# Four late MoE blocks: 32x32 turns on DVE and sixteen small array tiles instead of TensorE transposes

## The chip, the cores and the metric

The kernel runs on one core of a Trainium2 chip. The metric is the device time of one execution in microseconds (us). The engines are PE (TensorE: matmuls and weight loads), DVE (VectorE), ACT (ScalarE), POOL (GpSimd) and SP (SyncE, which here issues all DMAs from one in-order queue). Matmul results land in PSUM, which has 8 banks; everything else lives in SBUF.

## The reference

Three layers run one after another, all in float32.

```
attn = softmax(rope(q) rope(k)^T / 8) v        # 4 batches, 8 heads, 576 positions, 64 per head
x    = attn as [2304 tokens, 512]
h    = x @ w_in;  g = max(h,0) + alpha*min(h,0)     # [2304, 2048]
y    = g @ w_out                                    # [2304, 512]
logits = y @ phi                                    # [2304, 32 slots]
d = softmax of logits over the tokens;  slot_in = d^T @ y      # 32 slots: 8 experts x 4
slot_out[e] = relu(slot_in[e] @ w1[e]) @ w2[e]
out = softmax of logits over the slots @ slot_out
```

The kernel never forms y for all tokens. Since y = g @ w_out, the logits are g @ (w_out phi), and slot_in is (d^T g) @ w_out. So for each block of tokens it needs the sums over tokens of d (32 slots) times g (2048 features): the slots' sums. They are added up over the blocks with a running maximum, as in a streaming softmax.

## The kernel before

**Blocks.** The 2304 tokens are nine blocks of 256: two per batch (0 to 7) and one made of the four batches' last 64 tokens (8). A block's MoE work is 16 chunks of 128 features. A chunk is `mm1` (12 fp16 matmuls of 128x256 into the tile `ph`, line 734), then ACT `rl` (line 742) and DVE `g` (line 747), which read `ph` and free its PSUM bank. g then lies with features on the partitions and tokens along the free side. Three PSUM banks ("pm") serve `ph`, all transposes and most other results.

**Turning g.** The slots' sums contract over tokens, so tokens must lie on the partitions. After every second chunk PE makes four 128x128 transposes (`pt`, line 753) into a "pm" bank and ACT copies them to SBUF (`gt`, line 758): 8 such groups per block. After every fourth chunk come the logits (`lg`, line 764).

**Dispatch of a block** (`dispatch_events`): DVE scales the logits (`lp`, line 802), PE spreads them to 128 partitions (`lgt`, line 806), DVE takes the maximum (`sts`, line 827) and a copy (`lt`, line 816), ACT makes the fading factor (line 836) and the exponentials (`edt`, line 840), PE turns these (`pd`, line 845), DVE scales them (`dn`, line 850 or 852), PE makes the slots' sums (`pu`, line 858: 8 matmuls of 512 columns in four column tiles of the array, 32 slots by 512 features each), and DVE adds them to the running sum (`sacc`, line 867).

**After the last block**: `pa` turns the sum (line 1078), `at` scales it, `px` multiplies by w_out (line 1090), `pst` turns that (line 1100), and the experts follow: `ph` of line 1126 with w1, `po` of line 1180 with w2, and the output. The expert weights (33.5 MB) and w_out (8 MB) are fetched once attention has ended, into whatever SBUF tiles have come free: the pools "x" (26 tiles), "xt" (4), "w" (4) and "raw" (3 tiles, which also hold `gt`). w_out arrives as float64 and DVE converts it to fp32 in three operations for each of 16 pieces (`wo`, lines 986, 988 and 990).

**Order.** Every operation is given an engine, a cost, a due time, the operations it depends on and the buffers it takes. `Plan.order` plays this through with those costs and due times; the order in which operations start there becomes the program's order on each engine. On the chip each engine works through its list in order and waits on semaphores. MoE blocks run beside the attention of the next batch; when attention ends, part of block 5 and blocks 6 to 8 remain.

Of the kernel before, what the change touches and what calls it, by code (L numbers as in the profile page):

```python
# [11 lines left out]
F32 = mybir.dt.float32  # L12
# [3 lines left out]
ALU = mybir.AluOpType  # L16
AX = mybir.AxisListType
# [8 lines left out]
NS = E * SL  # L26
NT = B * S
BLK = 256
HALF = D // 2
NB, NW, WO_AT, MOVED = 13, 7, 12, 1  # L30

# [131 lines left out]
def attn_moe_softmoe(ctx, tc, qx, kx, vx, w_in, w_out, alpha, phi, w1, w2, tab, msks, w_out_t, out):  # L163
    nc = tc.nc
# [556 lines left out]
    def chunk_events(f, blk, due):  # L721
# [67 lines left out]
    def dispatch_events(ib, blk, due):  # L789
# [79 lines left out]
        def gather_s():  # L869
            if first:  # L870
                nc.vector.tensor_copy(ssum, st[:, 2:3])
            else:
                nc.vector.scalar_tensor_tensor(ssum, ssum, st[:, 1:2], st[:, 2:3], ALU.mult, ALU.add)

        s_e, s_pd, s_dn, s_pu = Slot("edt"), Slot("pm"), Slot("dn"), Slot("pm")
        s_lt, s_ln = Slot("lt"), Slot("pm")
# [7 lines left out]
        done.append(op(DVE, 131, d + 1, kept_l, [x], uses=[s_ln]))  # L884
        o = op(PE, 160, dp, turn_d, [o], takes=[s_pd], uses=[s_e, s_pd])
        o = op(DVE, 131, d, turned_d, [o], takes=[s_dn], uses=[s_pd, s_dn])
        o = op(PE, 1720, dp, slots, [o] + blk["gt_op"], takes=[s_pu], uses=[s_dn, s_pu] + list(blk["s_gt"].values()))
        a = op(DVE, 750, d, gather, [o, fd, run["sum"]], uses=[s_pu])
        run["gathered"] = a
        run["sum"] = op(DVE, 130, d, gather_s, [ex, fd, a])  # L890
        done.extend([a, run["sum"]])


    done = []
# [42 lines left out]
    for ib in range(9):  # L937
        if ib < 8:
            b, u = divmod(ib, 2)
            blk = {"x": xts[b, u], "inv": [(0, BLK, viv[b][:, 0:1])], "inv_op": [viv_op[b]]}  # L940
        else:
            blk = {"x": xts["tail"], "inv": [(64 * b, 64 * b + 64, viv[b][:, 0:1]) for b in range(B)], "inv_op": [tk_op]}
        blks.append(blk)
    for ib, blk in enumerate(blks):
# [24 lines left out]
    def late_w(f):  # L969
# [22 lines left out]
        d = 990 + 0.1 * f  # L992
        o = order_ops["wo"] = op(DMA, 1456, d, load, [att_done, order_ops.get("wo")], takes=[s_raw], uses=[s_raw])
        o = op(DVE, 450, d, lambda: conv(0), [o, wo_op.get(j)], takes=[] if z else [s_wo[j]], uses=u)
        o = op(DVE, 750, d, lambda: conv(1), [o], uses=u)
# [11 lines left out]
    for base in range(0, len(order), 4):  # L1007
        for half in range(2):
            for i in range(base, base + 4):
# [26 lines left out]
                for cut in range(n):  # L1036
                    due = 1000 + base + 2 * half + 0.2 * (i - base) + (2 * cut if n > 1 else 0)
                    ops.append(op(DMA, 1456 * len(parts) / n, due, lambda cut=cut, load=load: load(cut),
                                  [att_done, blks[8]["turn"] if slot.cls == "raw" else None] + ops[-1:],
                                  takes=[] if cut else [slot], uses=[slot]))  # L1040
# [27 lines left out]
    for j in range(2):  # L1068
        hz_zero.append(op(POOL, 900, 1000, lambda j=j: zero(j), [att_done], takes=[s_hz[j]], uses=[s_hz[j]]))
    sr = cst.tile([128, 2], F32, name="sr")  # L1070
# [4 lines left out]
    def turn_a():  # L1075
        fin["pa"] = ps_m.tile([128, 4, 4, NS], F32, tag="pm", name="pa")
        for c in range(4):
            nc.tensor.transpose(fin["pa"][:, c].rearrange("p g s -> p (g s)"), run["acc"][:, 128 * c:128 * c + 128], idf)

    def turned_a():  # L1080
        fin["at"] = fin["p"].tile([128, 4, 4, NS], F32, name="at")
        for c in range(4):
            iv = inv_w[:].rearrange("p (g h) -> p h g", h=2)[:, c // 2]
            nc.vector.tensor_tensor(fin["at"][:, c], fin["pa"][:, c], iv.unsqueeze(2).to_broadcast([128, 4, NS]), ALU.mult)

# [15 lines left out]

    o = op(PE, 430, D2 - 200, turn_a, [run["gathered"]], takes=[s_pa], uses=[s_pa])
    o = op(DVE, 600, FIRST, turned_a, [o, fin_open], uses=[s_pa])
# [303 lines left out]
```

## Time and profile before

| what | value |
|---|---|
| runs | 670.12, 674.26, 674.0 us; median 674.0 us |
| the profiled execution's own time | 673.49 us |
| its span, first to last instruction | 671.6 us |
| mean granted TensorE clock | 0.963 of full |
| PE busy | 611.0 us, 91% of the span |
| DVE busy | 456.0 us, 68% |
| ACT busy | 360.5 us, 54% |

The profile is one execution. Busy shares are means over stages: attention with MoE blocks beside it until about 508 us, then MoE blocks alone until about 600 us, then the dispatch of the last block, the experts and the output. What a change in one stage is worth has to be read from that stage: from the chain of waits (the work that ended last, followed back) and from the busy time of each engine in stretches of time. PEclk is the granted clock as a share of 2.4 GHz. The mean of a matmul's duration contains its way through the array, so matmuls that follow each other closely take less time than the sum of their durations. An fp32 matmul shows as two records in the trace.

### The profile page before, as it was taken

Reading aid. Unit: us, or ns where it says so; the run is one execution under the profiler, and the core shown is the slowest. Engines: PE = TensorE matmul, PEld = TensorE weight load, DVE = VectorE, ACT = ScalarE, POOL = GpSimd, SP = SyncE. Lnnn points to the kernel's source line nnn. Section 1 sums busy time; section 2 is a strip of 40 time slices with the busy share of each in tenths; the row PEclk is TensorE's granted clock in tenths of the full one; section 3 lists DMA queues with packets and bytes.
Section 4 is the critical chain, followed back from the end, with each engine's and each line's share of the span. In section 5 each row is a group of like instructions: output and inputs, shape, how many; then the busy total and the mean of one; then the engine's idle time right before and its main releaser. Section 6 shows DMA issues by size and latency. Waiting matters only on the chain.

```text
span 671.6 us, 13543 instructions
## 1 busy us (share of the span) xinstructions
PE 611.0 (91%) x5072; PEld 433.9 (65%) x5072; DVE 456.0 (68%) x989; ACT 360.5 (54%) x868; POOL 287.8 (43%) x283
## 2 busy tenths in 40 slices
PE   2879968979999999999999999999999999988984
PEld 1545444545888678686767868777776868753452
DVE  4776798787878777877576787677736884334332
ACT  2536545645687686775757676684643434330211
POOL 0698999374647656466353655522320000000000
PEclk9898988978999999999999999999999999999997
DMA  8954274530489796877867784777576984447998
GB/s 294 372 182 136 78 238 135 167 112 15 148 253 271 252 242 191 241 196 214 245 182 216 211 250 134 220 193 205 158 189 252 410 333 150 149 149 301 356 395 295
DMA packets 72672, 146.57 MB, mean 218 GB/s; under 512 B 8352, under 2 KB 37536, under 8 KB 72608
## 3 DMA queue, kind: packets, MB, share of 16 engines
q1 hardware_dynamic: 72608, 145.72, 68.3%
q8 instruction: 40, 0.66, 0.4%
q14 instruction: 24, 0.20, 0.1%
HBM read 108.73 MB, written 29.88 MB: 206 GB/s over the span
## 4 chain that ended last, share of the span: by engine, by line
PE 71%; DVE 9%; DMA 7%; POOL 6%; ACT 4%; SPq 2%; issue 2%; DVEq 0%; ACTq 0%; POOLq 0%
PE ph L734 26%; PE pv L573 13%; PE st L431 7%; PE pt L753 4%; DMA xw<-in_moe_w_dram 4%; PE lg L764 3%; PE pu L858 3%; POOL e L473 3%; PE st L418 3%; PE pt L494 2%; PE pc L537 1%; PE ph L1126 1%; PE rest L267 1%; DMA vt<-in_v_dram 1%; PE st L427 1%
## 5 line engine op out<-in xcount | busy, mean ns | idle before, releaser
L473 POOL TENSOR_SCALAR e<-e,mm 128x576 f32<-128x576 f32 x144 | 122.8, 865 | 152.7 <-DVE mm L449 112.1
L734 PE MATMUL ph<-xt,w 128*128 128x256 f16 x1536 | 184.5, 273 | 1.1 <-DVE g L747 0.4
L734 PEld LDWEIGHTS <-w 128*128 128x128 f16 x1728 | 163.9, 98 | 33.4 <-issue 11.8
L436 DVE TENSOR_REDUCE mm<-st 128x1 f32<-128x576 f32 x144 | 106.2, 742 | 27.6 <-PE st L431 21.4
L441 ACT ACTIVATE e<-st,mm 128x576 f32<-128x576 f32 x144 | 106.3, 739 | 29.4 <-DVE mm L436 26.5
L747 DVE SCALAR_TENSOR_TENSOR g<-rl,oma,ph 128x256 f32<-128x256 f32 x144 | 68.2, 474 | 59.6 <-ACT rl L742 59.0
L321 POOL TENSOR_TENSOR xn<-xn,tabs 128x576 f32<-128x576 f32 x60 | 90.3, 1519 | 30.6 <-DMA xn<-in_q_dram 14.9
L742 ACT ACTIVATE rl<-ph 128x256 f32<-128x256 f32 x144 | 55.0, 382 | 88.0 <-PE ph L734 87.6
L431 PE MATMUL st<-ks,qs 128*128 128x288 f32 x384 | 71.7, 314 | 0.3 <-ACT e L441 0.3
L481 DVE STREAM_TRANSPOSE tb<-e 128x512 f32<-128x512 f32 x96 | 66.6, 700 | 3.7 <-POOL e L473 3.0
L573 PE MATMUL pv<-ET,vt 128*64 128x256 f32 x512 | 63.9, 393 | 2.6 <-DVE qs L346 1.2
L418 PE MATMUL st<-ks 64*128 64x288 f32 (+1 forms) x168 | 46.9, 504 | 16.3 <-DVE ks L329 11.5
L431 PEld LDWEIGHTS st<-ks,qs 128*128 128x128 f32 x384 | 54.7, 191 | 4.7 <-issue 2.4
L758 ACT ACTIVATE gt<-pt 128x512 f32<-128x512 f32 x72 | 43.0, 597 | 15.7 <-PE pt L753 14.2
L573 PEld LDWEIGHTS pv<-ET,vt 128*64 128x64 f32 x512 | 35.6, 139 | 24.3 <-issue 6.1
L418 PEld LDWEIGHTS st<-ks 64*128 64x128 f32 (+1 forms) x168 | 26.7, 216 | 30.2 <-DVE ks L329 11.5
L753 PE MATMUL pt<-idf,g 128*128 128x128 f32 x288 | 43.8, 275 | 0.6 <-DVE g L747 0.4
L753 PEld LDWEIGHTS pt<-idf,g 128*128 128x128 f32 x288 | 33.3, 141 | 4.2 <-issue 1.2
L324 POOL TENSOR_TENSOR xn<-xn 128x576 f32<-128x576 f32 x24 | 35.6, 1482 | 0.9
L494 PE MATMUL pt<-idf,e 128*128 128x128 f32 x192 | 33.0, 306 | 3.3 <-POOL e L473 3.1
L494 PEld LDWEIGHTS pt<-idf,e 128*128 128x128 f32 x192 | 25.1, 159 | 15.1 <-POOL e L473 8.1
L349 ACT ACTIVATE ks<-xn 64x576 fp32r<-64x576 f32 x48 | 32.6, 680 | 0.7
(161 smaller groups left out, 840.2 us busy)
## 6 DMA issues: line engine op xcount, KB each, us to landing
sc<-tb SPq DMA_DIRECT2D x48, 512.0 KB, 4.3
ET<-sc SPq DMA_DIRECT2D x96, 256.0 KB, 5.4
xw<-in_moe_w_dram SPq DMA_DIRECT2D x42, 512.0 KB, 10.1
xn<-in_k_dram SPq DMA_DIRECT2D x16, 576.0 KB, 5.0
xn<-in_q_dram SPq DMA_DIRECT2D x16, 576.0 KB, 4.4
wraw<-in_moe_w_in_dram SPq DMA_DIRECT2D x8, 1024.0 KB, 7.1
wraw<-in_w_out_t_dram SPq DMA_DIRECT2D x8, 1024.0 KB, 5.4
wor<-in_moe_w_out_dram SPq DMA_DIRECT2D x16, 512.0 KB, 10.2
```

Of the source, the lines that this page charges most:

```text
L321: eng.tensor_tensor(e["x"][:, w], e["x"][:, w], tabs[:, (0 if z == "q" else 2) + w], ALU.mult)
L418: nc.tensor.matmul(st[to, j, at:at + w], x, k[rows, z:z + w], start=True, stop=True)
L431: nc.tensor.matmul(st[:, j, 0:288], r["q"][:, 768 * h + 128 * s:768 * h + 128 * s + 128].bitcast(F32R), r["k"][:, a, h, ks].bitcast(F32R), ...
L436: nc.vector.tensor_reduce(c["mm"][:, h:h + 1], c["st", h][:, :, 0:288], axis=AX.XY, op=ALU.max, negate=True)
L441: nc.scalar.activation(c["e"][:, h].rearrange("p (a n) -> p a n", a=2), c["st", h][:, :, 0:288], AF.Exp, bias=c["mm"][:, h:h + 1], accum_o ...
L473: nc.gpsimd.tensor_scalar(c["e"][:, h], c["e"][:, h], c["mm"][:, 6 + h:7 + h], 1.0, ALU.mult, ALU.mult)
L481: nc.vector.transpose(out=c["tb"][:, :, h].rearrange("p (q m) j -> p q m j", q=4), in_=c["e"][:, h, 64 * h:64 * h + 512].rearrange("p (m q ...
L494: nc.tensor.transpose(c["pt", h][:, i], c["e"][:, h, 64 * h + 128 * i:64 * h + 128 * i + 128], idf)
L573: nc.tensor.matmul(pv[r], v[k, 4 * h + i if i < 4 else 8], x, start=(i == 0), stop=(i == 4))
L734: nc.tensor.matmul(ph, wi[j][:, wp, kc, 128 * fo:128 * fo + 128], xt[:, xp, kc, :], start=(n == 0), stop=(n == 3 * KC - 1),)
L747: nc.vector.scalar_tensor_tensor(blk["g", j][:, fo, :], c["r"], oma[:, f:f + 1], c["ph"], ALU.mult, ALU.add)
L753: nc.tensor.transpose(c["pt"][:, t, i, :], blk["g", j][:, fo - 1 + i, 128 * t:128 * t + 128], idf)
```

## The change

In blocks 5 to 8 (`LATE = 5`) the transposes on PE and their copies on ACT go. DVE turns two chunks of g at a time with one 128x512 transpose that turns each 32x32 block by itself (`turn_g`, tile `gb`). Tokens then lie on the partitions only inside each strip of 32 partitions: strip a holds the features 32a to 32a+31 of each chunk of 128. So the slots' sums are made strip by strip: `slots_late` has 64 matmuls, each contracting over 32 tokens, on a 32x32 tile of the array. The tile's row strip a is the feature strip, its column strip the output's 32 partitions; the four row strips write into the four banks of the two score tiles ("st"), which attention no longer needs then. The eight groups of 32 tokens are split in pairs over two column strips, so each sum comes as two halves. The exponentials are scaled by DVE while still in rows (`scaled_d`) and turned by DVE too (`blocks_d`), in place of `pd` and `dn`. The running sum gets a new layout, `acc2` (in one of the four "xt" tiles, from the end of attention until `pa`), added to by four DVE operations per block; the first of the four blocks takes the old sum over. `pa` becomes eight matmuls that turn the sum and add the two halves, with a 0/1 matrix `selh`. Around this: the slots' sums of block 5 wait until attention is done (as `acc2` is opened then), one of the two zeroed tiles `hz` is made after `pa`, a w_out piece takes its "x" tile for the result when it is loaded, and expert weights in "raw" tiles may load once block 8 has taken its second `gb` tile.

```
-NB, NW, WO_AT, MOVED = 13, 7, 12, 1
+NB, NW, WO_AT, MOVED, LATE = 13, 7, 12, 1, 5
...
+        def turn_g():
+            if f == 1 or f == 9:
+                blk["gt", j // 2] = wgt.tile([128, 8, BLK], F32, tag="w", name="gb")
+            nc.vector.transpose(
+                out=blk["gt", j // 2][:, f % 8 - 1:f % 8 + 1, :].rearrange("p c n -> p (c n)"),
+                in_=blk["g", j][:, fo - 1:fo + 1, :].rearrange("p c n -> p (c n)"))
...
-        if fo % 2:
+        if fo % 2 and blk["late"]:
+            o = op(DVE, 760, due + 2.5, turn_g, blk["g_op"][-2:] + [raw_done, blk.get("turn")], takes=[s_gt] if f % 8 == 1 else [], uses=[s_g, s_gt])
...
+        def scaled_d():
+            for lo, hi, s in blk["inv"]:
+                nc.vector.tensor_scalar(c["et"][:, lo:hi], c["et"][:, lo:hi], s, None, ALU.mult)
+
+        def blocks_d():
+            nc.vector.transpose(out=c["lp"][:], in_=c["et"][:])
+
+        def slots_late():
+            pu = c["pu"] = [ps_s.tile([128, 2, 512], F32, tag="st", name="pu") for _ in range(2)]
+            for k in range(0, 8, 2):
+                for h in range(2):
+                    for r in range(2):
+                        to = slice(64 * h + 32 * r, 64 * h + 32 * r + 32)
+                        at = slice(32 * (k + r), 32 * (k + r) + 32)
+                        for a in range(4):
+                            rows = slice(32 * a, 32 * a + 32)
+                            nc.tensor.matmul(
+                                pu[a // 2][to, a % 2, 0:256], c["lp"][rows, at], blk["gt", h][rows, :, at],
+                                start=(k == 0), stop=(k == 6), tile_position=(32 * a, to.start))
+
+        def gather_late():
+            if ib == LATE:
+                run["acc2"] = xtp.tile([128, 8, 4, 32], F32, tag="xt", name="acc2")
+            for a in range(4):
+                src = c["pu"][a // 2][:, a % 2, 0:256].rearrange("p (c j) -> p c j", j=32)
+                dst = run["acc2"][:, :, a]
+                if ib > LATE:
+                    nc.vector.scalar_tensor_tensor(dst, dst, st[:, 1:2], src, ALU.mult, ALU.add)
+                    continue
...
+        if ib >= LATE:
+            o = op(DVE, 250 if ib < 8 else 400, d, scaled_d, [o], uses=[s_e])
+            o = op(DVE, 400, d, blocks_d, [o, lg], uses=[s_e, s_lp])
+            s_pu = [Slot("st"), Slot("st")]
+            o = op(PE, 1800, dp, slots_late, [o] + blk["gt_op"], takes=s_pu, uses=[s_lp] + s_pu + list(blk["s_gt"].values()))
...
+            a = op(DVE, 1700, d, gather_late, [o, a, run["sum"]], uses=s_pu + [s_acc2])
...
+    acc2_open = op(None, 0, 0, lambda: None, [att_done], takes=[s_acc2], uses=[s_acc2])
+    for blk in blks[LATE:]:
+        plan.also(blk["slots"], [acc2_open])
...
-        fin["pa"] = ps_m.tile([128, 4, 4, NS], F32, tag="pm", name="pa")
-        for c in range(4):
-            nc.tensor.transpose(fin["pa"][:, c].rearrange("p g s -> p (g s)"), run["acc"][:, 128 * c:128 * c + 128], idf)
+        fin["pa"] = ps_m.tile([128, 8, 2, NS], F32, tag="pm", name="pa")
+        for c in range(8):
+            nc.tensor.matmul(fin["pa"][:, c].rearrange("p h s -> p (h s)"), run["acc2"][:, c].rearrange("p a j -> p (a j)"),
+                             selh[:].rearrange("p h s -> p (h s)"), start=True, stop=True)
...
```

What this does to the order, at three places. **DVE while only MoE blocks run**, in block 8 (`g` is the chunk's second step, `gb` the new turn, `wo` the conversion of w_out; `dn`, `sacc` and `ssum` belong to the dispatch of block 7). Before:

```order
L747 SCALAR_TENSOR_TENSOR g<-rl,oma,ph 128x256
L850 TENSOR_SCALAR dn<-pd,vb 128x64
L747 SCALAR_TENSOR_TENSOR g<-rl,oma,ph 128x256
L867 SCALAR_TENSOR_TENSOR sacc<-sacc,sts,pu 128x512
L873 SCALAR_TENSOR_TENSOR ssum<-ssum,sts 128x1
L747 SCALAR_TENSOR_TENSOR g<-rl,oma,ph 128x256 x11
```

and now, in the last chunks of block 8:

```order
L747 SCALAR_TENSOR_TENSOR g<-rl,oma,ph 128x256
L763 STREAM_TRANSPOSE gb<-g 128x512
L1067 SCALAR_TENSOR_TENSOR wo<-wor,wo 128x512
L747 SCALAR_TENSOR_TENSOR g<-rl,oma,ph 128x256
L1063 TENSOR_SCALAR wo<-wor 128x512
L763 STREAM_TRANSPOSE gb<-g 128x512
L747 SCALAR_TENSOR_TENSOR g<-rl,oma,ph 128x256
L1065 SCALAR_TENSOR_TENSOR wo<-wor,wo 128x512
L747 SCALAR_TENSOR_TENSOR g<-rl,oma,ph 128x256
```

Before, the sixteen conversions were over well ahead of block 8, and `g` stood alone in DVE's list; now turns and conversions stand between the `g` up to the last chunk.

**DVE in the dispatch of block 8**, from the scaled logits to the running sum. Before:

```order
L802 TENSOR_SCALAR lp<-lg,vb 128x64 x4
L827 TENSOR_REDUCE sts<-lgt 128x1
L816 COPY lt<-lgt 32x256
L833 TENSOR_TENSOR sts<-sts 128x1
L824 COPY lall<-ln 128x64
L852 TENSOR_TENSOR dn<-pd,tailk 128x64
L1222 CAST idr<-idf 128x128
L867 SCALAR_TENSOR_TENSOR sacc<-sacc,sts,pu 128x512
```

and now, from the small `sts` on:

```order
L846 TENSOR_TENSOR sts<-sts 128x1
L1065 SCALAR_TENSOR_TENSOR wo<-wor,wo 128x512
L837 COPY lall<-ln 128x64
L1067 SCALAR_TENSOR_TENSOR wo<-wor,wo 128x512
L890 TENSOR_SCALAR edt<-edt,vb 128x64 x4
L1065 SCALAR_TENSOR_TENSOR wo<-wor,wo 128x512
L893 STREAM_TRANSPOSE lp<-edt 128x256
L1067 SCALAR_TENSOR_TENSOR wo<-wor,wo 128x512
L1063 TENSOR_SCALAR wo<-wor 128x512
L1065 SCALAR_TENSOR_TENSOR wo<-wor,wo 128x512
L1067 SCALAR_TENSOR_TENSOR wo<-wor,wo 128x512
L915 SCALAR_TENSOR_TENSOR acc_6270<-acc_6270,sts,pu 128x8x32 x4
```

The last three conversions now lie in this dispatch: two operations ahead of the scaling of the exponentials and one between the scaling and the turn.

**PE at the same place.** Before:

```order
L753 MATMUL pt<-idf,g 128x128 x8
L764 MATMUL lg<-g,wph 32x256 x4
L806 MATMUL lgt<-lp,sel_106 128x256
L821 MATMUL ln<-idf,lt 128x32 x2
L845 MATMUL pd<-idf,edt 128x32 x2
L858 MATMUL pu<-gt,dn 32x512 x8
L1078 MATMUL pa<-idf,sacc 128x128 x4
```

and now:

```order
L771 MATMUL lg<-g,wph 32x256 x4
L819 MATMUL lgt<-lp,sel_106 128x256
L834 MATMUL ln<-idf,lt 128x32 x2
L904 MATMUL pu<-gb,lp 32x256 x64
L1154 MATMUL pa<-selh,acc_6270 128x64 x8
L1169 MATMUL px<-wo,at 32x512 x16
```

The transposes `pt` and `pd` are gone from PE's list in blocks 5 to 8, `pu` has eight times as many matmuls of half the width, and `pa` twice as many.

## Rows read from the trace of the kernel before

**Rows 1.** The page: busy us, share of the span, instructions of PE.
```profile
PE 611.0 (91%) x5072; PEld 433.9 (65%) x5072; DVE 456.0 (68%) x989; ACT 360.5 (54%) x868; POOL 287.8 (43%) x283
```

**Rows 2.** The page: the chain that ended last, share of the span by engine.
```profile
PE 71%; DVE 9%; DMA 7%; POOL 6%; ACT 4%; SPq 2%; issue 2%; DVEq 0%; ACTq 0%; POOLq 0%
```

**Rows 3.** Busy time of each engine in stretches; columns as the first line says.
```profile
core 0: us, PE busy (x) PEld busy (x) DVE busy (x) ACT busy (x) POOL busy (x), PEclk, DMA share, GB/s
475.00:508.00 33.00, 32.85 (x310) 25.22 (x312) 16.33 (x37) 16.01 (x42) 8.40 (x12) 1.00 0.60 157
...
508.00:600.00 92.00, 90.36 (x830) 69.91 (x822) 54.62 (x120) 34.72 (x81) 0.00 (x0) 1.00 0.68 254
515.00:546.00 31.00, 30.18 (x281) 24.41 (x274) 25.73 (x57) 12.03 (x28) 0.00 (x0) 1.00 1.03 410
...
600.00:608.00 8.00, 4.59 (x22) 1.27 (x22) 2.76 (x11) 0.75 (x3) 0.00 (x0) 0.79 0.27 112
```

**Rows 4.** Chain of waits, 575 to 585 us: start us, us, what.
```profile
574.99 0.31 PE pd L845 x2
...
577.25 1.85 PE pu L858 x16
...
580.52 0.44 PE pt L753 x4
```

**Rows 5.** Groups of instructions: count, busy us, mean ns of one, idle before.
```profile
L753 PE MATMUL pt<-idf,g 128*128 128x128 f32 x288 | 43.8, 275 | 0.6 <-DVE g L747 0.4
...
L481 DVE STREAM_TRANSPOSE tb<-e 128x512 f32<-128x512 f32 x96 | 66.6, 700 | 3.7 <-POOL e L473 3.0 <-DMA sc<-tb 0.5
...
L747 DVE SCALAR_TENSOR_TENSOR g<-rl,oma,ph 128x256 f32<-128x256 f32 x144 | 68.2, 474 | 59.6 <-ACT rl L742 59.0
...
L867 DVE SCALAR_TENSOR_TENSOR sacc<-sacc,sts,pu 128x512 f32<-128x512 f32 x8 | 5.9, 741 | 2.0 <-PE pu L858 2.0
...
L986 DVE TENSOR_SCALAR wo<-wor 128x512 int32<-128x512 int32 x16 | 6.3, 420 | 1.2 <-DMA wor<-in_moe_w_out_dram 1.2
...
L988 DVE SCALAR_TENSOR_TENSOR wo<-wor,wo 128x512 int32<-128x512 int32 x16 | 10.8, 683 | 0.0
```

**Rows 6.** Timeline of PE at 59 and at 65 us: start us, us, what, count.
```profile
59.24 1.23 PE L418 MATMUL st<-ks 64*128 64x288 f32 x4
...
65.25 1.25 PE L418 MATMUL st<-ks 64*128 64x288 f32 x8
```

**Rows 7.** Chain of waits, 600 to 616 us: dispatch of block 8 and after.
```profile
600.00 0.87 DVE lp L802 x4
...
600.92 0.71 PE lgt L806 x2
...
601.65 0.42 DVE sts L827
602.08 0.32 DVE lt L816
...
603.92 3.36 PE pu L858 x16
...
608.30 0.67 PE pa L1078 x4
...
608.99 0.30 DVE at L1084
...
609.34 4.23 PE px L1090 x32
...
614.33 1.09 PE pst L1100 x8
```

**Rows 8.** Waits of SP's queue, 595 to 672 us: us in total, times, longest.
```profile
SPq L1033 <- PE pu L858: 9.0, 1, 9.0
SPq L1033 <- PE ph L1126: 7.3, 1, 7.3
```

More of the change, by code (lines that the diff above doesn't have):

```diff
@@ L779, in chunk_events @@
         blk["g_op"].append(o)
-        if fo % 2:
+        if fo % 2 and blk["late"]:
+            o = op(DVE, 760, due + 2.5, turn_g, blk["g_op"][-2:] + [raw_done, blk.get("turn")], takes=[s_gt] if f % 8 == 1 else [], uses=[s_g, s_gt])
+            blk["turn"] = o
+            blk["gt_op"].append(o)
+            if f == 9:
+                blk["turn9"] = o
+        elif fo % 2:
             s_pt = Slot("pm")
@@ L873, in gather_s @@
                 nc.vector.scalar_tensor_tensor(ssum, ssum, st[:, 1:2], st[:, 2:3], ALU.mult, ALU.add)
+        def scaled_d():
[24 more added lines that the diff above has]
+                    continue
+                for z in range(2):
+                    nc.vector.scalar_tensor_tensor(
+                        dst[:, 4 * z:4 * z + 4], run["acc"][:].rearrange("p (c a j) -> p c a j", a=4, j=32)[:, :, a], fz[:, z:z + 1],
+                        src[:, 4 * z:4 * z + 4], ALU.mult, ALU.add)
         s_e, s_pd, s_dn, s_pu = Slot("edt"), Slot("pm"), Slot("dn"), Slot("pm")
@@ L884, in dispatch_events @@
         done.append(op(DVE, 131, d + 1, kept_l, [x], uses=[s_ln]))
[L885 to L888, printed above, removed]
+        if ib >= LATE:
[3 more added lines that the diff above has]
+            o = op(PE, 1800, dp, slots_late, [o] + blk["gt_op"], takes=s_pu, uses=[s_lp] + s_pu + list(blk["s_gt"].values()))
+            blk["slots"] = o
+            a = fd
+            if ib == LATE:
+                a = op(DVE, 75, d, lambda: nc.vector.tensor_tensor(fz, parm, st[:, 1:2].to_broadcast([128, 2]), ALU.mult), [fd, parm_op])
+            a = op(DVE, 1700, d, gather_late, [o, a, run["sum"]], uses=s_pu + [s_acc2])
+        else:
+            o = op(PE, 160, dp, turn_d, [o], takes=[s_pd], uses=[s_e, s_pd])
+            o = op(DVE, 131, d, turned_d, [o], takes=[s_dn], uses=[s_pd, s_dn])
+            o = op(PE, 1720, dp, slots, [o] + blk["gt_op"], takes=[s_pu], uses=[s_dn, s_pu] + list(blk["s_gt"].values()))
+            a = op(DVE, 750, d, gather, [o, fd, run["sum"]], uses=[s_pu])
         run["gathered"] = a
@@ L891, in dispatch_events, with make_par @@
         done.extend([a, run["sum"]])
+    parm = cst.tile([128, 2], F32, name="parm")
+    fz = cst.tile([128, 2], F32, name="fz")
+    selh = cst.tile([128, 2, NS], F32, name="selh")
+    s_acc2 = Slot("xt")
+    def make_par():
+        nc.vector.memset(parm, 0.0)
+        for g in range(4):
+            nc.vector.memset(parm[32 * g:32 * g + 32, g % 2:g % 2 + 1], 1.0)
+    parm_op = op(DVE, 300, 60, make_par)
+    selh_op = op(DVE, 200, 60, lambda: nc.vector.tensor_reduce(
+        selh, idf[:].rearrange("p (h r s) -> p h s r", h=2, s=NS), axis=AX.X, op=ALU.add))
     done = []
@@ L942, in attn_moe_softmoe @@
             blk = {"x": xts["tail"], "inv": [(64 * b, 64 * b + 64, viv[b][:, 0:1]) for b in range(B)], "inv_op": [tk_op]}
+        blk["late"] = ib >= LATE
         blks.append(blk)
@@ L992, in late_w @@
         d = 990 + 0.1 * f
-        o = order_ops["wo"] = op(DMA, 1456, d, load, [att_done, order_ops.get("wo")], takes=[s_raw], uses=[s_raw])
-        o = op(DVE, 450, d, lambda: conv(0), [o, wo_op.get(j)], takes=[] if z else [s_wo[j]], uses=u)
+        o = order_ops["wo"] = op(DMA, 1456, d, load, [att_done, order_ops.get("wo")], takes=[s_raw] if z else [s_raw, s_wo[j]], uses=u)
+        o = op(DVE, 450, d, lambda: conv(0), [o, wo_op.get(j)], uses=u)
         o = op(DVE, 750, d, lambda: conv(1), [o], uses=u)
@@ L1038, in attn_moe_softmoe @@
                     ops.append(op(DMA, 1456 * len(parts) / n, due, lambda cut=cut, load=load: load(cut),
-                                  [att_done, blks[8]["turn"] if slot.cls == "raw" else None] + ops[-1:],
+                                  [att_done, blks[8]["turn9"] if slot.cls == "raw" else acc2_open if slot.cls == "xt" else None] + ops[-1:],
                                   takes=[] if cut else [slot], uses=[slot]))
@@ L1066, in zero @@
         nc.gpsimd.memset(fin["hz", j], 0.0)
-    for j in range(2):
-        hz_zero.append(op(POOL, 900, 1000, lambda j=j: zero(j), [att_done], takes=[s_hz[j]], uses=[s_hz[j]]))
+    hz_zero.append(op(POOL, 900, 1000, lambda: zero(0), [acc2_open], takes=[s_hz[0]], uses=[s_hz[0]]))
     sr = cst.tile([128, 2], F32, name="sr")
@@ L1100, in turn_s @@
             nc.tensor.matmul(fin["pst"][:, c], fin["xs"][:, 128 * c:128 * c + 128], sel4[:, 0], start=True, stop=True)
-    o = op(PE, 430, D2 - 200, turn_a, [run["gathered"]], takes=[s_pa], uses=[s_pa])
+    o = op(PE, 900, D2 - 200, turn_a, [run["gathered"], selh_op], takes=[s_pa], uses=[s_pa, s_acc2])
+    hz_zero.append(op(POOL, 900, 1000, lambda: zero(1), [o], takes=[s_hz[1]], uses=[s_hz[1]]))
     o = op(DVE, 600, FIRST, turned_a, [o, fin_open], uses=[s_pa])
```

4 lines of the change are left out of this document (3 added, 1 removed).

## The prediction

> **What bounds the kernel now.** I read the page first: PE is busy for 91% of the span [rows 1], and 71% of the chain that ended last is PE's [rows 2]. Both are means, so the stages come next. Between 475 and 508 us, where block 5 runs beside the last attention, PE is busy for 32.85 of 33.0 us. Between 508 and 600 us, MoE blocks alone, for 90.36 of 92.0 us, at full granted clock [rows 3]. In both stretches work that leaves PE's list should shorten the time, unless it uncovers another wait. From 600 us on it is different: PE works 4.59 of 8.0 us, and the chain there [rows 7] is a ladder of single operations that hand over between DVE, PE and ACT. What follows hangs on that ladder: SP's queue waits 9.0 us for block 8's `pu`, and later 7.3 us for the experts' first `ph`, before it can fetch more weights [rows 8]. So the end of the kernel moves with the ladder's end, us for us.
>
> **The change, part by part.** All sums are made against the profiled execution's own 673.49 us; the median of the runs shown is 0.5 us higher.
>
> *Transposes.* The 288 records of `pt` [rows 5] are 72 groups of four, 8 per block; four blocks lose 32 groups. One takes 0.44 us of the chain [rows 4]: 14.1 us. Of these, 24 groups (blocks 6 to 8) lie after attention and count fully: 10.6 us. The 8 of block 5 (3.5 us) lie beside attention, whose chain of maximum, exponential and transfers may wait where PE is lighter; I count 2.5. ACT's copies vanish too, worth nothing, as ACT is busy for 34.72 of 92 us [rows 3]. Blocks 5 to 7 also lose `pd`, 0.31 us each on the chain [rows 4]: 0.9.
>
> *The slots' sums.* Now 1.85 us per block [rows 4] for 16 records of 512 columns in four column tiles, four deep: 0.46 us each. The change has 64 matmuls, so 128 records of 256 columns, in sixteen tiles, eight deep. If all sixteen run at once this is 8 x 0.23 = 1.85 us again, and costs nothing. No row shows sixteen. Rows do show two row strips that write the same PSUM partitions in different banks: 4 records of the plain scores take 1.23 us, and 8 records, 4 in each row strip, take 1.25 us [rows 6]. A second strip cost nothing, and column tiles overlap already, so I take 1.85. The other ends: two strips at once 3.7 us, one strip at a time 7.4 us.
>
> The Trainium skill, TensorE: Matmul & The Clock Gate, section Measured speedup vs the span model, gives 10.6 times for sixteen tiles, not 16. By it the slots would take an estimated 64 x 0.46 / 10.6 = 2.8 us, and the sum below would be 4 us worse. The rows on two strips show no such loss.
>
> *DVE.* It gains, for 24 groups after attention, a 128x512 turn each, 0.70 us by the same operation on the exponentials [rows 5]: 16.8 us. The running sum becomes four operations of 256 columns, each like `g` (0.474 us), instead of 0.741 us: 1.2 us more per block, and 3.1 more in block 5, where eight operations take the old sum over. Three conversions (0.42 + 2 x 0.68 each [rows 5], 5.3 us in all) move on into the dispatch of block 8. Busy there was 54.6 us of 92 [rows 3]; now 54.6 + 16.8 + 3.1 + 2.4 - 5.3 = 71.6 in about 81. Who waits: the `g` that frees a `ph` bank now stands behind turns and conversions in DVE's list, and PE's next chunk needs that bank. There are three banks, so a `g` may be late by about a chunk before PE stops. I charge 1.0 us, with 0 and 5.8 as ends; the upper end is worked out as a rival below.
>
> *The ladder at the end.* Before, from `lp` to the start of `at`: 8.99 us [rows 7]. Now: `lp` 0.87, `lgt` 0.71, `sts` 0.42 and `lt` 0.32, as before: 2.3. Then DVE's list holds two conversion steps (2 x 0.68) ahead of the exponentials' scaling, beside ACT's work on the exponentials, which ends sooner: 1.4. The scaling in four pieces as for `lp`: 0.87. Another conversion step ahead of the turn: 0.68. The turn of 256 columns, half of 0.70: 0.35. The slots' sums at the rate that `pu` had here: 3.36, where the granted clock over the stretch was 0.79 [rows 3]. Four additions: 1.9. `pa` is 16 records with 128 columns of weights each, by `pst` (8 in 1.09 us): 2.2. Sum 13.1 us, so 4.1 more than before. If `pu` runs there as it does in warm stretches it is 2.6 more. If PE, with more waiting around it, is still at the lower clock in `pa` and `px` (4.23 us), these double and it is about 10 more; I take 4.1, since the same place before shows only `pu` slowed.
>
> *The rest.* Making `selh` and its like is some microseconds of DVE early on, where PE's chain leads; nothing. The DMA queue has the same bytes after attention; between 508 and 600 us it was busy for 0.68 of the time [rows 3], so fetches that now wait for later conversions have room, at the price of up to one fetch at the end, inside the ladder's bounds.
>
> *Sum.* 10.6 + 2.5 + 0.9 - 4.1 - 1.0 = 8.9 us less: 664.6 against 673.49, and 665 against the median of 674.0. The ends of this case: 661 (all of block 5's groups count, ladder 2.6, no bank waits) and 669 (half of them, ladder 6, bank waits 2).
>
> **The rivals.**
>
> *DVE sets the pace after attention.* For it: its list would be the fullest of all engines. Its densest stretch before held 25.73 us in 31 (0.83), with PE at 30.18 [rows 3]. Its 71.6 us after attention would take 86.3 at that share. PE's way is 92.0 - 10.6 - 0.9 = 80.5, so 5.8 us come back, of which the forecast holds 1.0: 670. Against it: durations of consecutive operations overlap a little, so 0.83 need not be the ceiling.
>
> *The ladder is dearer.* The lower clock holds through `pa` and part of `px`: 5 us more, 670. For it: PE has longer to wait between `lgt` and `pu` than before. Against it: `px` ran warm right after a slowed `pu` before.
>
> *The strips do not run at once.* This is the one that ends on the other side. If row strips shared something (a path into PSUM, the supply of columns), one strip at a time would make `pu` 7.4 us: 4 x 5.55 = 22 more than forecast, 687, slower than now. It decides from 4.1 us per `pu` on, where the four blocks have eaten the 8.9. If only two strips run at once, it is 7.4 us, 672. Against both stand the rows at 59 and 65 us.
>
> *More is gained.* PE's freed time beside attention also pulls chunks of later blocks forward, and the ladder is short: 659.
>
> **How the numbers follow.** Chances: forecast 0.50; DVE 0.17; dearer ladder 0.12; strips in pairs 0.05; strips one by one 0.10; more gained 0.06. The likeliest gives 665 us. Measured differences under about 1% (6.7 us) can't be told from none in this kernel, whose three runs spread by 0.6%. Faster than that means below 667.3: most of the forecast (0.43), the better case, and a few hundredths of the two at 670: 0.56. Slower, above 680.7: strips one by one and some of two bad cases together: 0.13. The rest, 0.31, is within 1%. The range 658 to 677 takes in the forecast with its ends, both cases at 670 and the pairs; it leaves out the strips one by one, the best of the better case and sums of two mishaps, just under 0.2.
>
> **What would show it.** Right: `pu` of blocks 5 to 7 with 128 records in about 1.9 us; no `pt` after block 4's; 81 to 83 us from attention's end to the last chunk; `lp` to `at` in about 13 us; SP's last long waits still on `pu` and `ph`. Wrong: `pu` of 4 us or more (strips); idle PE before `ph` put down to DVE `g`, with DVE busy for over nine tenths (DVE's pace); a PEclk of half over `px` (ladder); attention ending no sooner than at 508 us (block 5's share).

## The result and the profile after

The changed kernel took 681.06 us in the median of 4 runs (678.71 to 681.87), the kernel before 674.13 (670.12 to 674.27): a ratio of 1.0101, 95% interval 1.0063 to 1.0139. Run again later, beside 23 runs of the kernel before, it gave 676.84 us in 10 runs (674.15 to 680.85) and 1.0007 (0.9974 to 1.0040). Between no change and one per cent slower, then; nothing of the forecast 665 is there.

The profiled execution took 681.87 us, span 680.1. Its engine line and its chain by engine, as [rows 1] and [rows 2] had them:

```profile
PE 610.7 (90%) x5396; PEld 432.2 (64%) x5396; DVE 483.2 (71%) x1051; ACT 342.3 (50%) x836; POOL 287.6 (42%) x283
```

```profile
PE 64%; DMA 13%; DVE 10%; POOL 6%; SPq 3%; issue 2%; ACT 1%; ACTq 0%; DVEq 0%; POOLq 0%
```

PE fell from 71% of the chain to 64, and what came in its place is DMA, 7% before and 13% now. So some transfer is now waited for.

**Where attention ends.** Up to block 4's `pu`, PE's list is the same in both kernels. These rows give, for PE, a tile's records with the first and last start; they are of the kernel before (`pu` of block 4, the last `pv`), then the same two of the changed kernel.

```profile
L858 PE MATMUL pu<-gt,dn x16: 592/592/617, 457.1 to 458.4; 128*32 128x512 f32 x16
...
L573 PE MATMUL pv<-ec,vt x24: 376/402/427, 451.9 to 507.5; 64*64 64x256 f32 x24
```

```profile
L871 PE MATMUL pu<-gt,dn x16: 592/592/617, 459.5 to 460.8; 128*32 128x512 f32 x16
...
L573 PE MATMUL pv<-ec,vt x24: 376/402/427, 454.3 to 516.4; 64*64 64x256 f32 x24
```

From the last `pu` to the last `pv` it was 507.5 - 458.4 = 49.1 us, and is 516.4 - 460.8 = 55.6. (Why block 4 itself ends 2.4 us later is open: see the last section.) Attention, whose work the change does not touch, takes 6.5 us longer. The chain of waits at its end, changed kernel (start us, us, what):

```profile
498.69 0.48 DVE g L747
499.17 0.08 DVE mm L448
499.25 0.61 DVE gb L763
...
502.08 0.62 DVE tb L481
...
503.25 0.62 DVE tb L481
...
503.89 2.63 DMA sc<-tb
...
507.93 6.15 DMA ET<-sc
...
514.21 2.53 PE pv L573 x20
```

The last rows' exponentials are turned by DVE (`tb`), go out to DRAM, come back (`ET`) and only then make `pv`. Those turns now stand behind a `g`, a turn `gb` of block 5 and block 5's dispatch: the last `tb` starts 42.4 us after block 4's last record of `pu`, where it was 31.8. Busy time from that record's end to the end of attention, before and now (columns as in [rows 3]):

```profile
459.00:507.90 48.90, 48.75 (x447) 37.33 (x449) 27.51 (x63) 24.94 (x65) 12.81 (x18) 1.00 0.59 163
...
461.40:516.70 55.30, 51.55 (x446) 37.76 (x447) 36.43 (x82) 22.15 (x62) 11.86 (x17) 0.97 0.55 144
```

PE is idle for 3.75 us instead of 0.15: 1.9 for block 5's logits and dispatch, 1.5 for `ET`, 0.4 for `xt`. The other 2.8 us are more busy time: 16 chunks lie in this stretch where 14 did, and the `pv` that follows the idle time runs while the granted clock is down (0.66 from 504 to 508 us).

**The stages.** Busy time of each engine, changed kernel, columns as in [rows 3]:

```profile
464.00:516.70 52.70, 48.95 (x426) 36.36 (x426) 34.27 (x78) 22.04 (x62) 11.86 (x17) 0.97 0.56 141
516.70:597.70 81.00, 77.90 (x1030) 60.09 (x1028) 64.79 (x142) 19.04 (x52) 0.00 (x0) 1.00 0.69 263
597.70:600.00 2.30, 0.94 (x2) 0.30 (x2) 1.94 (x9) 0.00 (x0) 0.00 (x0) 0.76 1.02 417
600.00:618.00 18.00, 12.65 (x166) 9.95 (x170) 8.70 (x27) 0.75 (x3) 0.95 (x1) 0.50 0.73 240
```

The MoE stretch after attention is 81.0 us where it was 92 [rows 3]: here the change does what it was thought to do. One thing in it was not foreseen, a hole behind block 7's `pu` in which PE waits for nothing that the profile shows (the last section has more on it):

```profile
578.37 1.40 issue
```

Then comes the ladder, the chain of single steps from block 8's last logits to the experts. From 600 to 618 us its granted clock is 0.50, the lower of TensorE's two levels (1.2 GHz). Its chain, against [rows 7]:

```profile
597.76 0.75 DVE lp L815 x4
...
600.34 0.60 DVE wo L1065
600.94 0.14 DVE lall L837
601.08 0.60 DVE wo L1067
601.68 0.65 DVE edt L890 x4
602.33 0.60 DVE wo L1065
602.93 0.37 DVE lp L893
...
603.43 4.55 PE pu L904 x127
...
609.86 3.67 PE pa L1154 x16
...
613.96 6.58 PE px L1169 x32
...
622.77 10.46 PE ph L1206 x80
```

Besides the new steps, `px`, which the change does not touch, takes 6.58 us instead of 4.23, and the experts' first `ph` 10.46. SP's queue waits for what it waited for in [rows 8], and for `px` as well:

```profile
SPq L1110 <- PE ph L1206: 11.5, 1, 11.5
SPq L1110 <- PE px L1169: 8.1, 4, 6.1
...
SPq L1110 <- PE pu L904: 6.0, 2, 4.1
```

**All traces in one table.** For every kernel run: us from the start of the last record of block 4's `pu` to that of the last `pv` (attention's rest), on to that of block 8's last `lg` (MoE), on to the experts' first `ph` (ladder), on to the end of the span (experts). Each is a difference of two starts in that kernel's trace.

| kernel | attention's rest | MoE | ladder | experts | sum |
|---|---|---|---|---|---|
| before | 49.1 | 92.1 | 16.2 | 55.8 | 213.2 |
| changed | 55.6 | 80.4 | 26.0 | 57.3 | 219.3 |
| changed, again | 55.6 | 80.3 | 26.0 | 55.6 | 217.5 |
| blocks 6 to 8 only | 49.1 | 82.9 | 25.8 | 56.2 | 214.0 |
| blocks 7 and 8 only | 49.0 | 86.3 | 22.7 | 56.1 | 214.1 |
| conversions after the turn | 55.7 | 80.6 | 21.8 | 55.7 | 213.8 |
| waits filled | 55.5 | 80.3 | 20.1 | 55.8 | 211.7 |
| g by due time | 50.9 | 81.5 | 23.5 | 55.7 | 211.6 |
| matmuls cut in two | 55.5 | 95.6 | 26.3 | 55.7 | 233.1 |
| other order of matmuls | 55.4 | 80.5 | 25.4 | 55.7 | 217.0 |
| 6 to 8, filled | 49.0 | 83.0 | 20.1 | 55.4 | 207.5 |
| 6 to 8, filled, conversions | 49.1 | 82.9 | 19.1 | 56.4 | 207.5 |
| four blocks, all three edits | 51.0 | 81.5 | 20.8 | 55.6 | 208.9 |
| before, filled | 49.0 | 92.1 | 15.2 | 55.8 | 212.1 |

### The profile page after: what moved, and what is told of

It is laid out like the page before. It is cut to its first block, busy times and chain, and to the rows that moved or that the text cites. A ratio compares the mean times of both kernels' runs of the same rounds, so it can differ in the third digit from the quotient of the medians.

```text
span 680.1 us, 14229 instructions
## 1 busy us (share of the span) xinstructions
PE 610.7 (90%) x5396; PEld 432.2 (64%) x5396; DVE 483.2 (71%) x1051; ACT 342.3 (50%) x836; POOL 287.6 (42%) x283
## 4 chain that ended last, share of the span: by engine, by line
PE 64%; DMA 13%; DVE 10%; POOL 6%; SPq 3%; issue 2%; ACT 1%; ACTq 0%; DVEq 0%; POOLq 0%
PE ph L734 24%; PE pv L573 12%; PE st L431 6%; DMA ET<-sc 5%; DMA xw<-in_moe_w_dram 4%; PE st L418 3%; POOL e L473 2%; PE lg L771 2%; DMA sc<-tb 2%; PE pt L494 2%; PE pt L753 2%; PE pu L904 2%; PE ph L1206 2%; PE rest L267 1%; PE pc L537 1%
## 5 line engine op out<-in xcount | busy, mean ns | idle before, releaser
L436 DVE TENSOR_REDUCE mm<-st 128x1 f32<-128x576 f32 x144 | 106.3, 742 | 22.7 <-PE st L431 19.2
L573 PEld LDWEIGHTS pv<-ET,vt 128*64 128x64 f32 x512 | 37.1, 142 | 27.5 <-issue 8.9
L1143 POOL MEMSET hz<- 128x1024 f32 x2 | 1.9, 952 | 107.1 <-PE pa L1154 107.1
L583 ACT ACTIVATE xt<-pv,vb 128x256 f16<-128x256 f32 x32 | 15.1, 473 | 37.6 <-PE pv L573 37.5
L448 DVE TENSOR_SCALAR mm<-mm 128x2 f32<-128x2 f32 (+1 forms) x80 | 23.9, 299 | 10.7 <-ACT e L441 10.2
```

The costliest lines, as they stand in the source:

```text
L436: nc.vector.tensor_reduce(c["mm"][:, h:h + 1], c["st", h][:, :, 0:288], axis=AX.XY, op=ALU.max, negate=True)
L573: nc.tensor.matmul(pv[r], v[k, 4 * h + i if i < 4 else 8], x, start=(i == 0), stop=(i == 4))
```

## The experiments

They are called run 1 to run 12. Ratios are to the kernel before, run on the same chip between them, with 95% intervals. Edits are to the changed kernel unless said otherwise.

**1. Block 5 as before.**

```diff
-NB, NW, WO_AT, MOVED, LATE = 13, 7, 12, 1, 5
+NB, NW, WO_AT, MOVED, LATE = 13, 7, 12, 1, 6
```

> The new form only for blocks 6 to 8 (LATE = 6); block 5, which runs beside the last attention, is as it was before. Theory A (the planner's new order around block 5 keeps the last attention rows waiting): attention's last pv ends at 508 to 510 us again, not at 516.7. After it, the MoE blocks take 92.1 less two blocks' gain (2 x (3.5 + 0.3 - 0.8)), so about 86 us, and block 8's lp starts near 595 instead of 597.8. With the ladder as dear as in the changed kernel that is 677 to 679 us, with the transposes of block 5 back in. Rival B (attention is late for another reason that the change brings, such as the new constants made early or DVE's turns as such): the end stays at 514 us or later and the whole takes 683 us or more.

Ratio 0.9965 (0.9930 to 1.0000), median 675.01 us. Its rows of `pu` and `pv`:

```profile
L871 PE MATMUL pu<-gt,dn x16: 592/592/617, 458.4 to 459.7; 128*32 128x512 f32 x16
...
L573 PE MATMUL pv<-ec,vt x24: 376/402/427, 453.2 to 508.8; 64*64 64x256 f32 x24
```

508.8 - 459.7 = 49.1 us: attention's rest is what it was before, to the tenth. The early constants are still made here, so they are not the cause, and the new form of block 5 is. The time came out below the forecast of 677 to 679, since the MoE stretch is shorter than I had worked out: I had counted two late blocks, and it has three.

**2. Two late blocks (LATE = 7).**

> The new form only for blocks 7 and 8 (LATE = 7). Theory A with a late block worth about 3 us after attention (8 groups of 0.44, 0.3 for pd, less 0.8 because the slots' sums take 2.69 instead of 1.85): attention ends at 508 to 510 us as in the run with blocks 6 to 8, block 8's lp starts some 3 us later than there, and the time is some 3 us longer than there, 680 to 682 us, although it has half the change: nearly all of what the blocks gain is eaten by the ladder. Rival (a late block gains nothing, since DVE's turns or the sixteen tiles take back what the transposes gave): the same time as with blocks 6 to 8, or less.

Ratio 0.9994 (0.9965 to 1.0024), 675.60 us. The table gives a late block's worth: MoE of 92.1, 86.3 and 82.9 us with none, two and three late blocks, so 2.9 and 3.4 us each, as expected. The time did not grow by the 3 us expected, and the sum hardly (214.1 against 214.0), as the ladder of this kernel happens to be 3.1 us shorter, with no conversion in its chain. By the time alone the rival (a late block gains nothing) would stand; the MoE stretch rules it out.

**3. Conversions after the turn.**

```diff
+        hold = lambda step: [blks[8]["spread"]] if (f, step) >= (13, 0) else []
-        o = op(DVE, 450, d, lambda: conv(0), [o, wo_op.get(j)], uses=u)
+        o = op(DVE, 450, d, lambda: conv(0), [o, wo_op.get(j)] + hold(0), uses=u)
...
```

Steps 1 and 2 likewise; `spread` is block 8's turn of the scaled exponentials.

> All four blocks late, as in the changed kernel. The last nine conversion steps of the output weights wait until block 8's exponentials are turned, so that they run while PE makes pu and pa. Theory C1 (conversions in DVE's list lengthen the ladder): lp to the start of pu falls from 5.7 us to about 3.3 (four steps of 0.60 less), pu and pa stay as slow as they are (4.5 and 3.7), and the time falls by 2 to 2.5 us, to about 678.7. If the shorter wait also keeps TensorE at the higher clock, up to 5 us more. Rival: px must then wait for conversions, or the last weight fetches for their buffers, and the time stays within 1 us.

Ratio 1.0067 (1.0028 to 1.0106), 678.60 us: against the first 1.0101 that is 2.3 us less, as expected, but against the 1.0007 of run 10 it is nothing, so only the trace decides. Its ladder:

```profile
597.69 0.75 DVE lp L815 x4
...
600.85 0.75 DVE edt L890 x4
...
601.62 0.46 DVE lp L893
...
602.21 4.55 PE pu L904 x127
...
608.64 2.04 PE pa L1155 x16
```

From `lp` to `pu` 4.5 us instead of 5.7: 1.2 less, not 2.4, because ACT's exponentials stand there once DVE is free. `pu` is as slow as it was; `pa` took 2.04 us in this trace instead of 3.67. Over these two the stretches read:

```profile
602.20:606.70 4.50, 4.49 (x128) 2.72 (x128) 2.92 (x6) 0.00 (x0) 0.00 (x0) 0.50 0.24 68
...
608.60:611.00 2.40, 2.04 (x16) 1.86 (x16) 2.14 (x8) 0.00 (x0) 0.27 (x1) 0.89 0.82 299
```

So the same `pu` of 4.55 us comes with a third of the DMA that stood beside it in the changed kernel (share 0.24 here, 0.78 there), and the fast `pa` with a high granted clock. Why the clock rose ahead of `pa` here and not there, these runs do not show.

**4. PE's waits in the ladder filled.** The extra matmuls write a bank that nobody reads; they change no result.

```diff
+    def keep_warm(n, dep, due=3000.0):
+        s, e, o = Slot("pm"), {}, dep
+        ...
+            for _ in range(3):
+                nc.tensor.matmul(e["t"], xt[:, 0, 0, 0:128], xt[:, 0, 1, :], start=True, stop=True)
...
-            o = op(PE, 1800, dp, slots_late, [o] + blk["gt_op"], ...
+            hot = [keep_warm(9, lg)] if ib == 8 else []
+            o = op(PE, 1800, dp, slots_late, [o] + blk["gt_op"] + hot, ...
...
```

> All four blocks late, as in the changed kernel. Extra matmuls whose sums nobody reads fill PE's waits in the ladder: 12 (256 columns) before lgt, 27 before pu, 15 before pa, 6 before pst. Theory C2 (the ladder is dear because the clock granted falls to half while PE waits): the granted clock stays near 1.0 from 595 to 633 us; pu falls from 4.55 to about 2.7, pa from 3.67 to 1.9, px from 6.58 to 4.2, the experts' first ph from 10.46 to about 8.8, in all 6 to 8 us less: 673 to 675 us. Rival C3 (those durations come from sixteen tiles, short weights and the DMA that runs beside them, not from the clock): they stay within 10% and the time is the same or up to 2 us longer, because the extra matmuls stand in the way.

Ratio 0.9989 (0.9965 to 1.0014), 674.01 us. Two of its stretches and four steps of its chain:

```profile
596.60:600.00 3.40, 3.40 (x29) 2.59 (x27) 3.15 (x13) 0.75 (x3) 0.00 (x0) 1.00 1.02 418
600.00:614.30 14.30, 12.88 (x211) 8.85 (x208) 8.18 (x24) 0.00 (x0) 0.95 (x1) 1.00 0.74 260
```

```profile
602.21 2.79 PE pu L919 x116
...
606.97 1.98 PE pa L1170 x16
...
609.32 4.21 PE px L1185 x32
...
615.78 8.79 PE ph L1222 x80
```

The granted clock is 1.00 throughout, and `pu`, `pa`, `px` and `ph` are shorter by 1.76, 1.69, 2.37 and 1.67 us, 7.5 in all, with the same DMA beside them (share 0.74, 0.73 in the changed kernel). So it was the clock that made them slow, and not sixteen tiles, short weights or transfers; run 3, with no extra matmuls, points the same way. The ladder is 5.9 us shorter.

**5. Block 5's g by due time.** The planner writes each engine's list by due times; `g` has one that puts it ahead of every row's work.

```diff
-        o = op(DVE, 480, d, act, [o, oma_op], uses=[s_pm, s_r, s_g])
+        o = op(DVE, 480, due if blk is blks[LATE] and LATE == 5 else d, act, [o, oma_op], uses=[s_pm, s_r, s_g])
```

> All four blocks late, as in the changed kernel; only the due time of block 5's g (relu's second half, on DVE) is changed: it no longer stands ahead of everything in DVE's list but takes its turn among the attention rows' maxima and 32x32 turns. Theory A (the order that the planner writes for DVE and PE keeps the last rows waiting; here the part that g's rank has in it): the planner's own order then has attention end 4.3 us earlier than in the changed kernel, so the last pv ends near 512 us instead of 516.7; the MoE stretch after it stays 80 to 81 us and the ladder 16.2 us, so the whole is some 4 us shorter than the changed kernel, 676 to 678 us. Rival (what delays the rows is not the order but the load, DVE's turns beside the rows' work): the end of attention stays at 515 us or later and the time within 1 us of the changed kernel's.

Ratio 1.0002 (0.9968 to 1.0037), 674.42 us.

```profile
L871 PE MATMUL pu<-gt,dn x16: 592/592/617, 460.2 to 461.5; 128*32 128x512 f32 x16
...
L573 PE MATMUL pv<-ec,vt x24: 376/402/427, 455.0 to 512.4; 64*64 64x256 f32 x24
```

Attention's rest is 50.9 us: 4.7 of the 6.5 are gone, with all of DVE's turns still there. So it is the order and not the load of turns. One due time was edited, but the planner then writes PE's list anew too (17 chunks ahead of the last `pv`, not 16), so DVE's part is not shown apart. Busy time from block 4's `pu` to the end of attention:

```profile
462.10:512.70 50.60, 50.17 (x457) 37.51 (x457) 36.82 (x84) 22.14 (x63) 11.87 (x17) 1.00 0.61 157
```

PE's idle time is down to 0.43 us, at full clock: what is left of the 6.5, 1.8 us, is work of PE's that moved ahead of attention's end. The MoE stretch gains nothing from it (81.5 us), as the hole behind block 7's `pu` is 2.66 us here instead of 1.40, and the granted clock is down behind it (0.91 from 570 to 590 us). The time is below the 676 to 678 expected, as the ladder is shorter too (23.5 us, at 0.62 over `pu`).

**6. Each matmul of the slots' sums cut in two.**

```diff
-            for k in range(0, 8, 2):
+            for z, k in [(z, k) for z in range(2) for k in range(0, 8, 2)]:
...
-                                pu[a // 2][to, a % 2, 0:256], c["lp"][rows, at], blk["gt", h][rows, :, at],
+                                pu[a // 2][to, a % 2, 128 * z:128 * z + 128], c["lp"][rows, at], blk["gt", h][rows, 4 * z:4 * z + 4, at],
```

> All four blocks late; each of the 64 matmuls of the slots' sums is cut into two of 128 columns, so the same sums take 128 matmuls. Theory S1 (the sixteen tiles are held up by the time PE takes to start each matmul: 2.69 us for 128 records is 21 ns a record): pu takes about 5.4 us in blocks 5 to 7, and the whole is 8 to 11 us longer. S2 (columns set the time, sixteen tiles simply run at 11 times one tile): pu stays at 2.7 to 3.0 us, and the time within 2 us.

Ratio 1.0317 (1.0240 to 1.0393), 695.63 us. Block 5 in its chain:

```profile
514.50 3.05 PE pu L904 x169
517.55 4.21 issue
521.76 1.24 PE pu L904 x36
```

The same columns in twice the records take 8.5 us here where they took 2.69, 4.8 in block 6 and 7.7 in block 7, and the MoE stretch grows by 15 us. S2 (columns set the time) is out. But S1 does not come out either: without the holes (4.21, 1.18 and 3.05 us) the three take 4.3, 3.6 and 4.6 us, not 5.4. The starts in the trace show why: one round, a matmul on each of the sixteen tiles (32 records), follows the other after some 0.64 us at 256 columns and 0.42 at 128. So records and columns both count; each record has a weight load beside it, so these two are not told apart. What PE waits for in the holes, the profile does not name (see the last section).

**7. Another order of the 64 matmuls.**

```diff
-                for h in range(2):
-                    for r in range(2):
...
-                        for a in range(4):
+                for a in range(4):
+                    for h in range(2):
+                        for r in range(2):
```

> All four blocks late; the 64 matmuls of the slots' sums in another order: four in a row keep the row strip and the score bank and change the column tile, where the changed kernel has four in a row that keep the column tile and change the row strip. S1 (start time of each matmul) and S2 (columns) both leave pu at 2.7 us. S3 (some tiles wait for others because neighbours in the order share a column tile): pu moves by 0.3 us or more, to 1.9 us at best or 3.5 us and more at worst.

Ratio 1.0108 (1.0039 to 1.0176). From the first start to the last end, block 5's `pu` takes 2.754 us here and 2.755 in the changed kernel, and the MoE stretch is 80.5 us against 80.4: this order of neighbours makes no difference, and S3 is out.

**8. Edits 1, 3 and 4 together.** LATE = 6, four conversion steps held (from `(14, 2)`), waits filled.

> Three edits together: new form for blocks 6 to 8 only; the last four conversion steps of the output weights after block 8's turned exponentials; extra matmuls that nobody reads in PE's waits of the ladder (12, 21, 15 and 6). If the causes found so far add up: the run with blocks 6 to 8 gave 671.8 against a before of 674.1 by its ratio; the extra matmuls take off 7.6 (measured in the kernel with four late blocks), the conversions 1 to 2. That is 662 to 664 us, ratio 0.983 to 0.986. If the attention's order and the clock are the same loss seen twice, 668 us or more.

Ratio 0.9928 (0.9895 to 0.9961), 668.45 us, and by the table 5.7 us less than before (207.5 against 213.2): faster than both kernels, though less than expected. The sum in the table falls by 6.5 us from run 1, not 9: filling was worth 5.8 to 7.6 us (217.5 or 219.3 to 211.7), and what the conversions gave in the ladder came back behind it, where the experts' weights arrive.

**9. Edits 3, 4 and 5 with four late blocks.**

> All four blocks late, with three edits: block 5's g takes its turn by due time in DVE's list; the last six conversion steps of the output weights stand after block 8's turned exponentials; extra matmuls that nobody reads fill PE's waits in the ladder (12, 21, 15 and 6). From the end of block 4's slots' sums to the end of the program the traces so far have 213.5 us before, 219.6 in the changed kernel, 211.9 with g's place alone and 207.8 with blocks 6 to 8 and the ladder's two edits. If the losses are independent, g's place and the ladder's edits (some 4.4 us by those traces) give 207 to 208 us, that is 5.5 to 6.5 us less than before: ratio 0.990 to 0.993, no better than with blocks 6 to 8, since the fourth block's 3 us are eaten by attention's 2 us. If the order still holds back attention once the ladder is repaired, 211 us and a ratio near 1.

Ratio 0.9950 (0.9918 to 0.9981), 671.84 us, sum 208.9: a little over what independent losses give, and no better than three blocks. Its MoE stretch has a hole of 2.76 us behind block 7's `pu`, run 8's has none; without it the sum would be some 206 us (an estimate, 208.9 - 2.76).

**10. The changed kernel again.**

> The changed kernel once more, beside the same runs of the kernel before: the ratio should come out at 1.006 to 1.014 as the first time, and from block 4's slots' sums to attention's last pv its trace should show 55.7 to 55.9 us, as in every kernel with this order, although the start of the program moves by some 2 us from run to run.

The second half came true (55.6 us), the first did not (1.0007). The two intervals of the same kernel do not overlap, and the runs of one kernel spread by 1%: an interval holds for its own set of runs, and the ratio of four runs said too much. Differences of one stage are better read in the table.

**11. The kernel before, waits filled.** 12 extra matmuls ahead of block 8's `lgt`, 12 ahead of `pd`.

> The kernel before, with extra matmuls that nobody reads in block 8's ladder (12 before lgt, 12 between lgt and pd). Here the ladder has one slow place, pu in 3.36 us where the granted clock was about 0.58. If the extra matmuls only give back what the low clock cost, pu falls to 1.85 us and the time by about 1.5 us: ratio 0.998. The gain of the best version so far (0.9928) is then the change's own. Rival: the extra matmuls shorten anything that follows, whatever the ladder's form, and this kernel gains 4 us or more as well (0.994 or less).

Ratio 0.9962 (0.9934 to 0.9989), 672.49 us. `pu` fell from 3.36 to 1.99 us and the sum by 1.1. So filling is worth 1 us or a little more here, and 6 to 8 in the changed kernel, whose ladder has more for PE to do after each wait. Between this kernel and run 8 lie 4.6 us of trace: that is what the new form is worth in three blocks, once the waits are filled in both.

**12. Edits 1 and 4 without 3.**

> The new form for blocks 6 to 8 with the extra matmuls in the ladder's waits (12, 27, 15 and 6), conversions where the planner puts them. Beside the run that also moved the conversions (207.8 us from block 4's slots' sums to the end) this should have 1 to 2 us more between lp and pu: about 209 us, and a ratio of 0.993 to 0.996. If the conversions cost nothing once PE is kept busy, the same 207.8 and 0.993.

Ratio 0.9934 (0.9902 to 0.9965), 670.93 us, sum 207.5: the ladder is 1.0 us longer than in run 8, the experts 1.0 shorter. With PE kept busy the conversions cost nothing on the whole.

## Why the prediction was wrong

The sum of the forecast was 8.9 us less; between block 4's `pu` and the end, the trace shows 6.1 us more (219.3 - 213.2), and 4.3 when run again. Term by term:

*Transposes after attention, 10.6 and `pd` 0.9: right.* No `pt` comes after block 4's, and 2.9 to 3.4 us per late block are what 3.5 + 0.3 - 0.8 gives (runs 1 and 2).

*The 8 groups of block 5, "I count 2.5": this step failed, and in its sign.* I took work out of PE's list beside attention and asked only how much of it would not count. But the planner writes the lists anew: without the transposes, chunks of block 5 come forward (its last one starts 36 us after block 4's `pu` instead of 43), their `g` goes ahead of the rows' maxima and turns on DVE, the rows fall behind, and PE, out of chunks sooner, waits for block 5's dispatch and for the last rows, and then works at a lower clock. Attention takes 6.5 us longer. Of that, 2.7 come back: 45 chunks follow the last `pv` in PE's list instead of 47, at some 1.35 us each (12 records). So 3.8 us lost where 2.5 were to be gained. Run 1 shows that block 5's new form does it, run 5 that the order does. The prediction had this only as a sign to look for (attention ending no sooner than 508 us); as a rival with a price it was missing.

*Slots' sums at no cost: mis-sized.* 2.69 us per block instead of 1.85, 2.5 us over blocks 5 to 7:

```profile
518.16 2.69 PE pu L904 x117
```

The sixteen tiles do run at once: in the trace the first sixteen records start within 0.10 us and take 0.40 each, and the rival at 687 us needed 4.1 us per `pu`. But a round on all sixteen comes every 0.64 us, not every 0.46, as 1.85 us for four rounds would have it. The two row strips of [rows 6] have 4 and 8 records, too few to show that. By the Trainium skill (TensorE: Matmul & The Clock Gate, section Measured speedup vs the span model) the estimate was 2.8 us; this case's trace agrees with it at 256 columns, and I should have let it stand against my two rows. Run 6 shows that the agreement does not carry to 128 columns, where the same columns took 3.6 us and more even without the holes.

*DVE's stalls, 1.0: right in size.* PE waits 1.1 us for DVE's `g` in the MoE stretch, against 0.4 before. DVE is busy for 64.79 of 81.0 us, less than the 71.6 forecast; DVE's pace is not the bound.

*The ladder, "I take 4.1": mis-sized, 9.8 measured (26.0 - 16.2).* I priced `pu` at the lower clock, and `pa` and `px` at the higher, "since the same place before shows only `pu` slowed". At the lower clock `pu` took 4.55 instead of 3.36, `pa` 3.67 instead of 2.2 and `px` 6.58 instead of 4.23: 5.0 of the 5.7 us that were missing. The prediction had that size in hand ("about 10 more") and set it aside; as the rival "the ladder is dearer" it stood at 0.12 and 5 us. Run 4 shows that the clock alone is worth 5.9 us there. What remains of the ladder with filled waits, 20.1 against 16.2, is 3.9 us; that this is close to the forecast 4.1 is partly luck, as the forecast holds a slow `pu`, and for a fast one it gave 2.6. The experts' first `ph`, 1.67 us slower in the first trace and not in the second, is the last piece.

Together, against before: -10.6 - 0.9 + 2.5 + 3.8 + 9.8 + 1.5 (experts) = +6.1, as measured. It closes a little too well: the MoE stretch also holds the hole of 1.4 us and 0.7 us more waiting for `g`, which no term above has, and against them two savings that none has either, block 5's `lgt` and `ln` (0.7 us), which now run before attention ends, and a wait of 0.8 us for `edt`, which is gone.

## What to carry to other kernels

Where a planner writes the order, work that leaves one engine's list beside a long chain can change the order of all lists: compare in the new order who now stands ahead of that chain on every engine, and price a delay of it as a rival. A ladder of single steps is priced at both clocks, with the untouched steps behind it: before, the clock was back at full level right behind `pu`, now only while `px` ran. Filling the waits with matmuls that nobody reads is a cheap test, and here a repair. Many small array tiles are priced by their number of records as well as by columns, and from a run with as many.

## What the runs showed of the hardware

In the changed kernel the granted clock was 0.50 from 600 to 618 us, with PE busy for 12.65 of 18 us; with filled waits it was 1.00 from 600 to 614.3, with 12.88 of 14.3. Before, it was below full level only around `pu` (0.58 from 604 to 606 us, 0.57 from 606 to 608).

The 128 records of a `pu` in sixteen tiles, 256 columns each, start within 2.38 us: the first sixteen 6.7 ns apart, those of later rounds mostly 16 to 17 ns, with pauses of 0.12 to 0.19 us in between. The Trainium skill (TensorE: Matmul & The Clock Gate, section Wait — 56ns, not 53.3ns?) says that start-to-start never drops below about 25 ns; records on different tiles start closer than that here.

The holes have a common sign. In the twelve traces of kernels with late blocks, PE stands idle for 0.9 us or more with nothing to wait for eleven times after 440 us: four times in run 6, inside `pu`, and once in each of the other seven traces with four late blocks, behind block 7's `pu` (1.24 to 2.76 us). Each time a packet of 16 KB of the queue that the page lists as `q8 instruction` had landed 1.26 to 1.59 us before PE went on; that queue has 40 packets before, 43 in the changed kernel and 47 in run 6, rising as PE's list does. Kernels with three late blocks or fewer show no such hole. That PE waited for its instructions is a guess that fits all eleven; no run tried it.

At the end of block 4, which lies between 456.8 and 465.0 us in 14 traces, PE's list has been the same in all kernels. Most of the spread arises in the first 240 us. The eight traces of kernels with four late blocks have a mean of 461.4 us and the other six of 458.3; whether the change has a part in that is open, and the sums in the table leave it out.
